# Two small edits to a fused attention and MLP kernel: a cast layout for whole-array transposes, and a second PSUM tile for one A@V

## The chip, the cores and the metric

The kernel runs on one core of one Trainium2 chip. The metric is device time in microseconds (us). It varies from one execution to the next, so it is given as a median with the range. The span in a profile, first to last instruction, is 1.8 us shorter than the device time of the same execution (390.1 against 391.87 for the profiled execution of the kernel before).

Names: PE is TensorE, PEld its weight loads, DVE is VectorE, ACT is ScalarE, POOL is GpSimd, SP is the engine that issues most DMAs. PSUM is the memory that holds the tiles PE writes in this kernel, and from which DVE and ACT copy them; such a copy is called an eviction. Tiles in the profile: `qraw` and `qe` are q before and after its cast, `tps` its transposes, `sc` and `sch` scores, `av` and `avh` the product A@V of attention and v, `xT` that product scaled, `hps` and `ops` the two MLP layers. The chain is the work that ended last, followed back from wait to wait; a load lands when its data has arrived.

## The reference

```python
scores = scale * q @ k.T                  # 8 batches, 12 heads, 448 positions, 64 wide
attn   = maximum(scores, 0)**2 / 448
x      = (attn @ v), heads side by side   # 3584 x 768
h      = x @ w_in                         # 768 x 2048
g      = maximum(h, 0) + alpha * minimum(h, 0)
out    = g @ w_out                        # 2048 x 768
```

## The kernel before

The heads are worked on four at a time, as 24 "quads" (three to a batch). Two heads lie on partitions 0 to 63 and two on 64 to 127; the index `s` tells the two heads of a partition half apart. Scores are computed transposed, so q and k of a quad are first turned by PE (quads 0 to 5) or by a DMA (the rest).

The opening: q and k of quad 0 are loaded as fp32, cast on DVE and ACT, turned, and the first scores follow. Quads 1 to 5, and quad 0's v, are loaded with a casting DMA from POOL's queue.

```python
raw[(0, w)]  = raw_pool.tile([128, 2, NJ, D], F32, ...)
cast[(0, w)] = early_pool.tile([128, 2, NJ, D], BF16, ...)     # s outside, j inside
...
warm(15)                                     # 15 empty matmuls
nc.vector.tensor_copy(cast[(0, "q")][:, 0], raw[(0, "q")][:, 0])
nc.scalar.copy(cast[(0, "q")][:, 1], raw[(0, "q")][:, 1])
transpose(0, "q")
nc.scalar.copy(cast[(0, "k")][:, :, :3], raw[(0, "k")][:, :, :3])
transpose(0, "k", first, nc.scalar)
warm(2)
nc.vector.tensor_copy(cast[(0, "k")][:, :, 3:], raw[(0, "k")][:, :, 3:])
scores(0, 0); scores(0, 1); scores(0, 2, "both", mm_ps)
```

Inside `transpose`, each j takes two half-width transposes, one per s, which write the two partition halves of PSUM:

```python
for j in js:
    for s in range(2):
        nc.tensor.transpose(ps[64 * s:64 * s + 64, j], t[:, s, j], ident)
```

The end of batch 1's attention: `attnv(5)` multiplies quad 5's attention with v into one PSUM tile, and one ACT instruction scales it into `xT`. Twelve matmuls of the first MLP layer that need only quads 3 and 4 stand ready around it, four of them after it. Then come those that need quad 5.

```python
# in attnv, batch 1 and later
elif isinstance(ps, list):      # two PSUM tiles
    nc.vector.tensor_scalar(xT[b][:, g, 0], half[0][:, :S], out_scale, None, ALU.mult)
    nc.scalar.activation(xT[b][:, g, 1], half[1][:, :S], ACTF.Copy, scale=out_scale)
else:                           # one tile
    nc.scalar.activation(xT[b][:, g], ps[:, :, :S], ACTF.Copy, scale=out_scale)
...
ffn1(1, 0, range(0, 4))
ffn1(1, 1, range(0, 4))
attnv(5)
feed(7, "v")()                  # DVE casts quad 7's v
ffn1(1, 2, range(0, 4))         # the four matmuls that don't need quad 5
for ff in range(3):
    ffn1(1, ff, range(4, KM))   # these need it
```

Of the kernel before, what the change touches and what calls it, by code (L numbers as in the profile page):

```python
# [11 lines left out]
BF16 = mybir.dt.bfloat16  # L12
# [8 lines left out]
NJ = 7  # L21
# [3 lines left out]
def kernel(  # L25
# [10 lines left out]
    nc = tc.nc  # L36
    B, H, S, D = q.shape
    d_model, d_ff = moe_w_in.shape
    assert H * D == d_model and S == PP * NJ and D == 64 and H % 4 == 0
    NG = H // 4  # L40
    n_pe = 2 * NG
# [6 lines left out]
    def pool(name, bufs, **kw):  # L48
        return ctx.enter_context(tc.tile_pool(name=name, bufs=bufs, **kw))
# [6 lines left out]
    early_pool = pool("early", 2)  # L56
# [15 lines left out]
    ident = singles.tile([128, 128], BF16)  # L72
# [4 lines left out]
    raw, cast, qT, kT, vb = {}, {}, {}, {}, {}  # L77
    src = {"q": q, "k": k, "v": v}

    def flat(n, w):  # L80
        b, g = quads[n]
        return src[w][b, 4 * g:4 * g + 4].rearrange("(s hf) (pp j) d -> (hf pp) s (j d)", hf=2, j=NJ)

    def load(n, names="qkv", after=None):
        for w in names:
            t = raw_pool.tile([128, 2, NJ, D], F32, tag=w, name=f"{w}raw")
            raw[(n, w)] = t
            if after is not None:
                nc.gpsimd.tensor_copy(t[:, 0, 0, 0:1], after)
                after = None  # L90
            nc.sync.dma_start(out=t.rearrange("p s j d -> p s (j d)"), in_=flat(n, w))
# [10 lines left out]
    def copy(eng, o, i):  # L102
        if eng is nc.scalar:
            nc.scalar.copy(o, i)  # L104
        else:
            eng.tensor_copy(o, i)  # L106

    def to_bf16(n, w, eng):
        r = raw.pop((n, w))
        if w == "v":  # L110
            t = v_pool.tile([128, 2, NJ, D], BF16, tag="v", name="vb")
            vb[n] = t
            copy(eng, t, r)
        else:
            t = cast_pool.tile([128, NJ, 2, D], BF16, tag=w, name=f"{w}b")
            cast[(n, w)] = t
            copy(eng, t.rearrange("p j s d -> p s j d"), r)

    def transpose(n, w, js=range(NJ), eng=None):
        store = qT if w == "q" else kT  # L120
        if n not in store:
            store[n] = qkT_pool.tile([128, NJ, 2, PP], BF16, tag=w, name=f"{w}T")
        t, dst = cast[(n, w)], store[n]
        if n >= n_pe:
            nc.sync.dma_start_transpose(out=dst.rearrange("p j h c -> p j (h c)"),
                                        in_=t.rearrange("p j s d -> p (j s d)"))
            return
        ps = mm_ps.tile([128, NJ, 2 * PP], BF16, tag="mm", name="tps")
        for j in js:
            for s in range(2):  # L130
                nc.tensor.transpose(ps[64 * s:64 * s + 64, j], t[:, s, j], ident)  # L131
        lo, hi = js[0], js[-1] + 1
        copy(eng or nc.vector, dst[:, lo:hi].rearrange("p j h c -> p j (h c)"), ps[:, lo:hi])
# [54 lines left out]
    def squares(keep=0, single=None):  # L188

        while len(todo) >= 2 + keep or todo and single is not None:  # L190
            m = min(len(todo), 2)
            some = [todo.pop(0) for _ in range(m)]
            t = some[0][2]
            a = at_pool.tile([128, 2, 2, S], BF16, tag="at", name="at")
            if m == 2:
                nc.vector.tensor_tensor(a, t, t, ALU.mult)  # L196
            else:
                cur.clear()
                if single is nc.scalar:
                    nc.scalar.activation(a[:, 0], t[:, 0], ACTF.Square)  # L200
                else:
                    nc.vector.tensor_tensor(a[:, 0], t[:, 0], t[:, 0], ALU.mult)
            for i, (n, j, _) in enumerate(some):
                att[(n, j)] = a[:, i]
# [3 lines left out]
    def attnv(n, js=range(NJ), space=sc_ps, apart=False):  # L208
        b, g = quads[n]
        if js[0] == 0:  # L210
            if space is mm_ps:
                av_ps[n] = [mm_ps.tile([128, 512], F32, tag="mm", name="avh") for _ in range(2)]
            elif apart:
                av_ps[n] = [sc_ps.tile([128, 2, 512], F32, tag="sc", name="av2")[:, 0] for _ in range(2)]
            else:
                av_ps[n] = sc_ps.tile([128, 2, 512], F32, tag="sc", name="av")
        ps = av_ps[n]
        half = ps if isinstance(ps, list) else [ps[:, r] for r in range(2)]
        for j in js:
            a = att.pop((n, j))  # L220
            for r in range(2):
                for s in range(2):
                    nc.tensor.matmul(half[r][64 * s:64 * s + 64, :S],  # L223
                                     vb[n][64 * r:64 * r + 64, s, j, :],
                                     a[64 * r:64 * r + 64, s],
                                     start=(j == 0), stop=(j == NJ - 1))
        if js[-1] != NJ - 1:
            return
        if g == 0:
            xT[b] = xT_pool.tile([128, NG, 2, S], BF16, tag="xT", name="xT")  # L230
        if b == 0:
            nc.scalar.activation(xT[b][:, g, 0], half[0][:, :S], ACTF.Copy, scale=out_scale)  # L232
            if g > 0:
                nc.vector.tensor_scalar(xT[b][:, g, 1], half[1][:, :S], out_scale, None, ALU.mult)
            else:
                nc.scalar.activation(xT[b][:, g, 1], half[1][:, :S], ACTF.Copy, scale=out_scale)
        elif isinstance(ps, list):
            nc.vector.tensor_scalar(xT[b][:, g, 0], half[0][:, :S], out_scale, None, ALU.mult)  # L238
            nc.scalar.activation(xT[b][:, g, 1], half[1][:, :S], ACTF.Copy, scale=out_scale)  # L239
        else:  # L240
            nc.scalar.activation(xT[b][:, g], ps[:, :, :S], ACTF.Copy, scale=out_scale)  # L241
# [62 lines left out]
    def steps(b, what):  # L304
        if what == "in":
            return [(1.12, lambda ff=ff: ffn1(b, ff)) for ff in range(KF)]
        cs = range(0, 3) if b % 2 == 0 else range(3, 7)
        return [(1.3, lambda c=c, hf=hf, h=h: ffn2(b // 2, c, hf, h)) for c in cs for hf in range(2) for h in range(2)]


    NQ = len(quads)
    def group(units, how="both"):

        def f():
            order = sorted(units, key=lambda u: u[1] == "av")
            for i, (n, j) in enumerate(order):
                if j == "av":
                    if (n, NJ - 1) not in att:
                        squares(single=nc.vector)
                    attnv(n)  # L320
                elif i == 0 and len(order) == 3:
                    scores(n, j, how, mm_ps)
                else:
                    scores(n, j)
            squares()
            for n, j in order:
                if n < n_pe:
                    continue
                if j == 0:
                    if n + 2 < NQ:  # L330
                        load(n + 2)
                    if n + 1 < NQ:
                        transpose(n + 1, "k")
                        transpose(n + 1, "q")
                if j == 4 and n > 2 * NG and n + 2 < NQ:
                    for w in "kqv":
                        to_bf16(n + 2, w, nc.gpsimd)
        return f


# [5 lines left out]
    def warm(count):  # L346

        ps = sc_ps.tile([128, 2, 512], F32, tag="sc", name="warm")
        for _ in range(count):
            nc.tensor.matmul(ps[:, 0, :256], warm_w, warm_x, start=True, stop=True)  # L350

    nc.scalar.dma_start(out=alpha_sb, in_=moe_alpha.rearrange("(kf p) -> kf p", p=128))
    for w in "qk":
        raw[(0, w)] = raw_pool.tile([128, 2, NJ, D], F32, tag=w, name=f"{w}raw")
        cast[(0, w)] = early_pool.tile([128, 2, NJ, D], BF16, tag=w, name=f"{w}e")
    first, rest = range(0, 3), range(3, NJ)
    nc.sync.dma_start(out=raw[(0, "q")].rearrange("p s j d -> p s (j d)"), in_=flat(0, "q"))
    for js in (first, rest):
# [10 lines left out]
    load_bf16(0, "v")  # L369
    load_bf16(1, "v")  # L370
    warm(15)
    nc.vector.tensor_copy(cast[(0, "q")][:, 0], raw[(0, "q")][:, 0])
    nc.scalar.copy(cast[(0, "q")][:, 1], raw[(0, "q")][:, 1])
    transpose(0, "q")
    nc.scalar.copy(cast[(0, "k")][:, :, :3], raw[(0, "k")][:, :, :3])
    transpose(0, "k", first, nc.scalar)
    warm(2)
    nc.vector.tensor_copy(cast[(0, "k")][:, :, 3:], raw[(0, "k")][:, :, 3:])
    scores(0, 0)
    scores(0, 1)  # L380
    scores(0, 2, "both", mm_ps)
# [1 line left out]
    ps = mm_ps.tile([128, KF], F32, tag="mm", name="aps")  # L383
# [75 lines left out]
    f = [fn for _, fn in steps(0, "in")]  # L459
# [8 lines left out]

    ffn1(1, 0, range(0, 4))
    ffn1(1, 1, range(0, 4))  # L470
    attnv(5)
    feed(7, "v")()
    ffn1(1, 2, range(0, 4))
    for ff in range(3):
# [107 lines left out]
```

## Time and profile before

| | kernel before |
|---|---|
| device time, 3 executions | 391.43 us (391.19 to 391.59) |
| span in the profile | 390.1 us |
| PE busy, DVE, ACT | 97%, 65%, 55% |
| first matmul of the MLP (hps) starts | 22.22 us |
| last A@V matmul of batch 1 starts | 72.70 us |

The chain and timeline lines that the argument starts from stand in the prediction.

### The profile page before, as it was taken

The numbers are of one execution on the slowest core, as the hardware profiler recorded it, in microseconds if no ns is written. First come the engines' busy times: TensorE is split into PE (matmuls) and PEld (weight loads), VectorE is DVE, ScalarE is ACT, GpSimd is POOL, SyncE is SP. The second block draws the span as 40 slices with busy tenths as digits, with TensorE's granted clock in tenths as the row PEclk, the third lists the DMA queues.
The fourth block names the chain that finished last, engine by engine and source line by source line (L and its number), as shares of the span: only waits on it lengthen the run. The fifth ranks groups of instructions, "written<-read, shape, count | busy, mean of one in ns | idle before, by whom it ended". The sixth has DMA issues, their size and how long they took to land.

```text
span 390.1 us, 7871 instructions
## 1 busy us (share of the span) xinstructions
PE 379.2 (97%) x3210; PEld 215.0 (55%) x3210; DVE 252.1 (65%) x335; ACT 215.6 (55%) x361; POOL 73.3 (19%) x88
## 2 busy tenths in 40 slices
PE   7699999999999999999999999999999999999996
PEld 4345556445665456645665456654566545655564
DVE  3976877587677757766674666777676376725411
ACT  5975767574556656654474645766565365624200
POOL 5664000061241014201231012311030000000000
PEclk9999999999999999999999999999999999999999
DMA  7999997893995528926494354947163220130033
GB/s 155 185 208 205 203 221 271 239 319 83 237 271 184 114 76 232 229 64 165 87 276 141 66 164 96 247 159 172 30 91 85 72 47 2 42 81 2 0 82 81
DMA packets 64755, 55.43 MB, mean 142 GB/s; under 512 B 35776, under 2 KB 60496, under 8 KB 64720
## 3 DMA queue, kind: packets, MB, share of 16 engines
q1 hardware_dynamic: 53472, 44.77, 44.2%
q0 software_dynamic: 10976, 9.96, 16.1%
q8 instruction: 25, 0.41, 0.4%
q10 hardware_dynamic: 272, 0.21, 0.2%
q14 instruction: 10, 0.08, 0.1%
HBM read 45.62 MB, written 11.01 MB: 145 GB/s over the span
## 4 chain that ended last, share of the span: by engine, by line
PE 94%; DMA 3%; ACT 1%; DVE 1%; issue 0%
PE hps L255 37%; PE ops L271 37%; PE avh L223 7%; PE sc L156 6%; PE sch L156 3%; DMA ke<-in_k_dram 2%; PE ops L294 1%; PE tps L131 1%; PE av L223 1%; DMA qraw<-in_q_dram 1%; ACT rl L185 1%; ACT xT L241 0%; DVE gT L263 0%; ACT rl L163 0%; DVE rl L165 0%
## 5 line engine op out<-in xcount | busy, mean ns | idle before, releaser
L255 PE MATMUL hps<-xT,w_in_sb 128*128 128x448 bf16 x768 | 149.3, 353 | 0.8 <-ACT xT L232 0.4
L271 PE MATMUL ops<-w_out_sb,gT 128*128 128x384 bf16 x864 | 145.8, 326 | 0.0
L263 DVE SCALAR_TENSOR_TENSOR gT<-neg,beta_sb,hps 128x448 bf16<-128x448 f32 x128 | 85.7, 679 | 61.1 <-ACT neg L262 60.2
L271 PEld LDWEIGHTS <-gT 128*128 128x128 bf16 x864 | 83.4, 98 | 61.2 <-issue 7.9
L255 PEld LDWEIGHTS <-w_in_sb 128*128 128x128 bf16 x768 | 74.0, 98 | 72.8 <-issue 5.9
L262 ACT ACTIVATE neg<-hps 128x448 f32<-128x448 f32 x128 | 69.0, 545 | 63.8 <-PE hps L255 63.7
L185 ACT ACTIVATE rl<-sc 128x896 bf16<-128x896 f32 x87 | 77.1, 923 | 44.4 <-PE sc L156 44.3
L196 DVE TENSOR_TENSOR at<-rl 128x1792 bf16<-128x1792 bf16 x80 | 85.5, 1112 | 2.1 <-ACT rl L185 0.9
L106 DVE COPY osb<-ops 128x384 f32<-128x384 f32 x30 | 16.7, 557 | 46.0 <-PE ops L271 46.0
L163 ACT ACTIVATE rl<-sch 128x448 bf16<-128x448 f32 x81 | 41.6, 550 | 4.6 <-PE sch L156 4.6
L106 POOL CAST kb<-kraw 128x896 bf16<-128x896 f32 x16 | 18.4, 1152 | 115.2 <-DMA kT<-kb 55.7
L156 PE MATMUL sc<-qT,kT 64*64 64x448 bf16 x456 | 35.9, 355 | 3.8 <-ACT rl L185 1.5
L223 PE MATMUL avh<-at,vb 64*64 64x448 bf16 x588 | 34.2, 350 | 0.0
L156 PEld LDWEIGHTS <-kT 64*64 64x64 bf16 x672 | 21.9, 106 | 20.1 <-issue 13.0
L104 ACT COPY osb<-ops 128x384 f32<-128x384 f32 x24 | 11.4, 475 | 36.0 <-PE ops L271 36.0
L223 PEld LDWEIGHTS <-vb 64*64 64x64 bf16 x672 | 25.6, 106 | 9.3 <-issue 4.9
L183 DVE TENSOR_SCALAR rl<-sc 128x896 bf16<-128x896 f32 x27 | 29.4, 1090 | 0.6 <-PE sc L156 0.6
L106 POOL CAST vb<-vraw 128x896 bf16<-128x896 f32 x16 | 16.8, 1050 | 36.5 <-PE avh L223 36.0
L156 PE MATMUL sch<-qT,kT 64*64 64x448 bf16 x216 | 22.5, 355 | 0.0
L106 POOL CAST qb<-qraw 128x896 bf16<-128x896 f32 x16 | 15.9, 991 | 32.3 <-DMA qT<-qb 32.3
L165 DVE TENSOR_SCALAR rl<-sch 128x448 bf16<-128x448 f32 x27 | 16.8, 622 | 2.6 <-ACT xT L239 0.8
L238 DVE TENSOR_SCALAR xT<-avh 128x448 bf16<-128x448 f32 x19 | 11.9, 625 | 7.7 <-PE avh L223 7.7
(55 smaller groups left out, 96.8 us busy)
## 6 DMA issues: line engine op xcount, KB each, us to landing
out_dram<-osb SPq DMA_DIRECT2D x54, 192.0 KB, 2.7
qraw<-in_q_dram SPq DMA_DIRECT2D x19, 448.0 KB, 5.4
kraw<-in_k_dram SPq DMA_DIRECT2D x18, 448.0 KB, 4.4
vraw<-in_v_dram SPq DMA_DIRECT2D x18, 448.0 KB, 6.3
w_out_sb<-in_moe_w_out_dram POOLq DMA_DIRECT2D x2, 1536.0 KB, 20.0
w_in_sb<-in_moe_w_in_dram POOLq DMA_DIRECT2D x8, 192.0 KB, 8.3
w_in_sb<-in_moe_w_in_dram POOLq DMA_DIRECT2D x4, 384.0 KB, 9.7
vb<-in_v_dram POOLq DMA_DIRECT2D x6, 224.0 KB, 9.7
```

The source lines that it names most:

```text
L106: eng.tensor_copy(o, i)
L156: nc.tensor.matmul(half[r][64 * c:64 * c + 64, :S], kT[n][64 * r:64 * r + 64, j, c, :], qT[n][64 * r:64 * r + 64, :, c, :], start=True, st ...
L163: nc.scalar.activation(rl[:, r], half[r][:, :S], ACTF.Relu)
L165: nc.vector.tensor_scalar(rl[:, r], half[r][:, :S], 0.0, None, ALU.max)
L183: nc.vector.tensor_scalar(rl, ps[:, :, :S], 0.0, None, ALU.max)
L185: nc.scalar.activation(rl, ps[:, :, :S], ACTF.Relu)
L196: nc.vector.tensor_tensor(a, t, t, ALU.mult)
L223: nc.tensor.matmul(half[r][64 * s:64 * s + 64, :S], vb[n][64 * r:64 * r + 64, s, j, :], a[64 * r:64 * r + 64, s], start=(j == 0), stop=(j ...
L255: nc.tensor.matmul(ps, w_in_sb[:, km // 2, km % 2, bass.ts(ff, 128)], xT[b][:, km // 2, km % 2, :], start=(km == 0), stop=(km == KM - 1))
L262: nc.scalar.activation(neg, ps, ACTF.Relu, scale=-1.0)
L263: nc.vector.scalar_tensor_tensor(gT[b // 2][:, ff, (b % 2) * S:(b % 2) * S + S], neg, beta_sb[:, ff:ff + 1], ps, ALU.mult, ALU.add)
L271: nc.tensor.matmul(ps, gT[sb][:, ff, bass.ts(c, 128)], w_out_sb[:, ff, bass.ts(hf, 384)], start=(ff == 0), stop=(ff == KF - 1))
```

## The change

The intent: quad 0's casts write `p j s d` in place of `p s j d`, so that the two s-tiles of one j lie side by side and one 128-wide transpose does what took two of 64. And the last A@V of batch 1 goes into two PSUM tiles, so that DVE and ACT can take one half each. A loop in `group`, which served quads that never reach it, is removed.

```diff
+        if n == 0:
+            t = t.rearrange("p j s d -> p j (s d)")
 ...
         for j in js:
+            if n == 0:
+                nc.tensor.transpose(ps[:, j], t[:, j], ident)
+                continue
             for s in range(2):
 ...
-        cast[(0, w)] = early_pool.tile([128, 2, NJ, D], BF16, ...)
+        cast[(0, w)] = early_pool.tile([128, NJ, 2, D], BF16, ...)
 ...
-    nc.vector.tensor_copy(cast[(0, "q")][:, 0], raw[(0, "q")][:, 0])
-    nc.scalar.copy(cast[(0, "q")][:, 1], raw[(0, "q")][:, 1])
+    nc.vector.tensor_copy(cast[(0, "q")][:, :, 0], raw[(0, "q")][:, 0])
+    nc.scalar.copy(cast[(0, "q")][:, :, 1], raw[(0, "q")][:, 1])
 ...  (both casts of k likewise)
-    attnv(5)
+    attnv(5, apart=True)
```

More of the change, by code (lines that the diff above doesn't have):

```diff
@@ L325, in f @@
             squares()
-            for n, j in order:
-                if n < n_pe:
-                    continue
-                if j == 0:
-                    if n + 2 < NQ:
-                        load(n + 2)
-                    if n + 1 < NQ:
-                        transpose(n + 1, "k")
-                        transpose(n + 1, "q")
-                if j == 4 and n > 2 * NG and n + 2 < NQ:
-                    for w in "kqv":
-                        to_bf16(n + 2, w, nc.gpsimd)
         return f
@@ L354 @@
         raw[(0, w)] = raw_pool.tile([128, 2, NJ, D], F32, tag=w, name=f"{w}raw")
-        cast[(0, w)] = early_pool.tile([128, 2, NJ, D], BF16, tag=w, name=f"{w}e")
+        cast[(0, w)] = early_pool.tile([128, NJ, 2, D], BF16, tag=w, name=f"{w}e")
     first, rest = range(0, 3), range(3, NJ)
@@ L371 @@
     warm(15)
-    nc.vector.tensor_copy(cast[(0, "q")][:, 0], raw[(0, "q")][:, 0])
-    nc.scalar.copy(cast[(0, "q")][:, 1], raw[(0, "q")][:, 1])
+    nc.vector.tensor_copy(cast[(0, "q")][:, :, 0], raw[(0, "q")][:, 0])
+    nc.scalar.copy(cast[(0, "q")][:, :, 1], raw[(0, "q")][:, 1])
     transpose(0, "q")
-    nc.scalar.copy(cast[(0, "k")][:, :, :3], raw[(0, "k")][:, :, :3])
+    nc.scalar.copy(cast[(0, "k")][:, :3].rearrange("p j s d -> p s j d"), raw[(0, "k")][:, :, :3])
     transpose(0, "k", first, nc.scalar)
     warm(2)
-    nc.vector.tensor_copy(cast[(0, "k")][:, :, 3:], raw[(0, "k")][:, :, 3:])
+    nc.vector.tensor_copy(cast[(0, "k")][:, 3:].rearrange("p j s d -> p s j d"), raw[(0, "k")][:, :, 3:])
     scores(0, 0)
```

## The prediction

The sum came to 391.43 - 0.28 + 0.0 = 391.15 us. That DVE's cast of q would grow from 0.43 us to 0.63 in the new layout was the author's estimate. Beside it stood a measured time, 0.62 us for a 448-column DVE pass out of PSUM in the trace of the kernel before. What is said of a change of tiling rests on one measurement: 0.28 us from the last av matmul (64x64) to the next hps matmul (128x128), against 0.189 between two hps matmuls.

> **What bounds the kernel now.** I read the page first (busy shares, chain, groups), then the chain in order of time, then the timeline around the two places that the change touches.
>
> The page's busy shares and its chain by engine:
>
> ```profile
> PE 379.2 (97%) x3210; PEld 215.0 (55%) x3210; DVE 252.1 (65%) x335; ACT 215.6 (55%) x361; POOL 73.3 (19%) x88
> ...
> PE 94%; DMA 3%; ACT 1%; DVE 1%; issue 0%
> ```
>
> TensorE is busy 97% and holds 94% of the chain. The same matmuls run after the change, so only a wait of PE, or a switch between its tilings, can be won. The granted clock is 1.00, so nothing is to be had there. The groups of the stretch from 74.1 us on show no idle time of PE before any group but the one wait at 74.07 itself: everything there is back to back. So a wait removed before 74.1 us should arrive at the end whole, and one moved into a place where PE waits for something else should not arrive at all.
>
> The chain in order of time shows the two places. Columns: start us, length us, what.
>
> ```profile
> 0.74 3.87 DMA qraw<-in_q_dram
> 4.61 0.02 issue
> 4.63 0.44 DVE qe L372
> 5.07 0.04 issue
> 5.12 0.99 PE tps L131 x20
> 6.10 0.02 issue
> 6.13 0.49 ACT kT L104
> ...
> 8.31 7.40 DMA ke<-in_k_dram
> 15.71 0.04 issue
> 15.76 0.58 PE tps L131 x14
> ...
> 71.60 1.48 PE av L223 x28
> 73.08 0.02 issue
> 73.10 0.93 ACT xT L241
> 74.03 0.04 issue
> 74.07 3.00 PE hps L255 x15
> ```
>
> The first is quad 0's cast and transposes, which the change rewrites. But the chain then goes through the load of quad 2's keys, landing at 15.71. The second is the last A@V of batch 1: its result leaves PSUM in one ACT instruction of 0.92 us, and PE's next-but-four matmul waits for it.
>
> The timeline of the second place (start us, us, engine, line, operation, then idle before and who ended it):
>
> ```profile
> 72.98 0.93 PE L255 MATMUL hps<-xT,w_in_sb 128*128 128x448 bf16 x4
> 73.10 0.92 ACT L241 ACTIVATE xT<-av 128x896 bf16<-128x896 f32 x1 [3.42 <-PE av L223]
> ...
> 74.07 1.49 PE L255 MATMUL hps<-xT,w_in_sb 128*128 128x448 bf16 x7 [0.16 <-ACT xT L241]
> ```
>
> PE has only four matmuls that don't need this result. The page counts 0.16 us idle, but that is measured from the modelled end of a pipelined matmul. A matmul of 448 columns in a stream follows its predecessor after 0.189 us (96 of them in one run take 18.16 us later in the same chain: 0.189). Four from 72.98 (the first gap is 0.20) let the fifth start at 73.75. It starts at 74.07. The real loss is **0.32 us**.
>
> [...]
> - [...] The trace has such a stream, the last 128-column pieces of the output, each with its own 128x128 load: 10 in 0.72 us with 219 ns for one, so (0.72 - 0.22) / 9 = 55.7 ns. [...]
> - [...] the 14 half-width transposes take 0.58 us, which is 7 pairs at 56 ns (below), so the two column halves already run at once. [...] between the last av matmul and the first hps about 0.09 us is lost beyond the normal pitch.
> [...]
>
> **Part 1: quad 0's layout.** What it removes: 14 of 28 transposes with their loads. Does it remove time? Timeline of such transposes now and of full-width 128-column matmuls:
>
> ```profile
> 8.82 0.58 PE L131 MATMUL tps<-ident,ke 128*64 128x128 bf16 x14
> ...
> 385.60 0.72 PE L294 MATMUL ops<-w_out_sb,gT 128*128 128x128 bf16 x10
> ```
>
> Seven full-width ones at 55.7 ns with 20 ns of start-up like the present ones take 6 x 0.0557 + 0.02 + 0.22 = 0.57 us; the 14 half-width ones take 0.58. So the instruction count halves and **PE's time does not**. The first q pair now starts half at 5.12 (DVE's half) and half at about 5.25 (ACT's); the rest stream from 5.25. The merged ones start when both halves are cast, 5.25, and end the same.
>
> What it adds: [...] I choose 0.63. It then ends at 5.26, not 5.06, against ACT's half at 5.20: the transposes of q start 0.06 late. q's copy to SBUF would end at 6.55 in place of 6.49; the k side (ACT cast to 5.67, three pairs of transposes, ACT copy to 6.61) ends later than that and barely moves (up to 0.03 us, if the q transposes push the k ones). ACT's casts cost the same in either layout (961 strided, 966 plain, for 128x896). The rest of k, cast by DVE with an even split, has 0.4 us of room. So the first score starts at 6.66 to 6.69. The switch of tiling before the two warm-up matmuls goes, 0.1 us, but the scores behind them wait for kT anyway.
>
> And whatever comes of it meets the wait for quad 2's keys:
>
> ```profile
> 14.00:16.00 2.00, 1.42 (x36) 0.89 (x26) 1.90 (x3) 2.00 (x5) 0.00 (x1) 1.00 1.22 191
> ...
> 15.76 0.58 PE L131 MATMUL tps<-ident,ke 128*64 128x128 bf16 x14 [0.58 <-DMA ke<-in_k_dram]
> ```
>
> The first line is the stretch 14 to 16 us (busy PE, PEld, DVE, ACT, POOL, clock, DMA share, GB/s): the DMA engines are full, so that transfer lands when the queue reaches it, not 7.4 us after its issue. PE waits 0.58 us there, and so stands ready to absorb up to that much delay, and to swallow any gain. **Part 1: 0.0 us**, give or take 0.1.
>
> **Part 2: two PSUM tiles.** Removed: one ACT pass of 917 ns. Added: DVE 625 ns and ACT 543 ns at the same time (the means of the groups of other batches that leave PSUM in halves). DVE starts a little behind PE's end, 0.04 after ACT in the one place of the kernel before where two tiles of this pool are used (26.56 and 26.60): 73.12 + 0.625 = 73.75, and 0.04 for the semaphore gives 73.79 for the fifth matmul, in place of 74.07. Gain **0.28 us**; 0.04 of the 0.32 us stays. Second PSUM tile: its last reader, a score pass at 67.9 + 0.95 = 68.9 us, is done long before 71.53, so nothing waits. DVE is idle from 71.6 to 75.2; the cast of quad 7's v, which it does now at 70.97, moves behind the eviction to about 73.75 to 74.37. Its buffer is asked for again by the load issued at about 75.98, so that doesn't wait either.
>
> **Part 3: the loop taken out of the grouped scores** handled only quads from 6 on, and the groups are called with quads 3 to 5 alone. It never ran: 0.
>
> **Sum:** 391.43 - 0.28 + 0.0 = **391.15 us**.
>
> **The rivals.**
> - The start counts after all. For it: the chain does name the first cast and transposes. Against: seven pairs cost what seven full ones do, and the load at 15.71 hides the rest. If it held and some 0.3 us fell away there as well: 390.85.
> - The DVE cast slows down and this is not absorbed, because DVE is nearly without gaps from 7.5 to 16.5 us (1.90 of 2.00 in the stretch above). [...] Against: 0.58 us of PE's waiting comes after it, and the k side sets the first score. It would give back up to 0.2: 391.35.
> - The stall at 74 us only changes its name: half the result now waits on DVE, and if DVE's eviction began late (behind a cast) PE would wait for DVE as it did for ACT. For it: two casts and an output copy sit in DVE's queue just before. Against: they end by 71.1. It would make 391.4.
>
> **Range and chances.** Three runs before span 0.40 us, larger than the effect, so the measured median may be 0.2 either way; the rivals reach from 390.85 to 391.4. I choose 390.7 to 391.6. Two per cent would be 7.8 us; all that the changed code touches on the path is under 2 us. Within 2%: 0.98, the other two 0.01 each.
>
> **What would show it.** Right: the fifth hps matmul after the last av of batch 1 waits for DVE, under 0.1 us, and what follows lies some 0.28 us earlier to the end; the seven-transpose groups take about 0.57 us; the q cast on DVE takes 0.6 us or more; quad 2's keys still land near 15.7. Wrong: those keys landing clearly earlier or later, seven transposes in 0.35 us or in 0.75, PE idle anew after 74 us, or a span that moves by more than 0.6 us.

## More of the kernel before

PE is the engine that everything waits for, but not from the start: until 22 us the scores wait for loads, casts and for the copies out of PSUM. From there on it runs nearly without gaps (busy 363.7 of the 367.9 us that are left). One row of the page matters later. In it each digit is the granted TensorE clock, in tenths, of one fortieth of the span (9.75 us):

```profile
PEclk9999999999999999999999999999999999999999
```

No slice is below 9. The row, and the mean clock that is given for each execution below, leave out the start, though: the clock records begin at 4.16 us here, and before that the empty matmuls of 256 columns follow each other after 0.213 us, against 0.120 us for the pair at 6.02. So neither shows a slow start.

## The result

| | before | after |
|---|---|---|
| device time, 6 executions each | 391.36 us (391.17 to 391.85) | 391.42 us (390.98 to 393.20) |
| ratio of the means, 95% interval | | 1.0008 (0.9988 to 1.0028) |
| span of the profiled execution | 390.1 us | 391.3 us |

The ratio is the mean time of one kernel's fast executions over that of the other's of the same rounds, so it is not quite the ratio of the medians. All executions here count as fast (none is 1.5% above the fastest).

The medians agree, and yet the six executions of the changed kernel hold 390.98, which is under every one of the kernel before, and 393.20 and 392.22, which are above. The profiled one is the 393.20. So the first question is what happened in that execution. The same row of its page as above, and the chain by engine:

```profile
PEclk9699999999999999999999999999999999999999
...
PE 95%; DMA 2%; ACT 1%; POOL 0%; issue 0%; DVE 0%
```

The second slice has a 6: for part of it PE's clock was halved. The clock records of the trace say it exactly: 0.5 from 11.11 to 17.94 us, 6.83 us long. The same 28 A@V matmuls of quad 0 (timeline: start us, us, engine, line, operation, count), in the kernel before:

```profile
13.66 1.52 PE L223 MATMUL avh<-at,vb 64*64 64x448 bf16 x28
```

and in the changed kernel:

```profile
14.12 2.88 PE L228 MATMUL avh<-at,vb 64*64 64x448 bf16 x28
```

They take nearly twice as long. Nothing in the diff touches them. The chain of the changed kernel, in order of time:

```profile
4.88 5.58 DMA qe<-in_q_dram
10.46 0.04 issue
10.50 0.58 PE tps L136 x14
...
14.39 2.61 PE avh L228 x27
...
73.19 1.45 PE av L228 x28
74.64 3.71 PE hps L260 x19
```

Two things differ from the chain that the prediction shows. The load of quad 2's keys is not on it (here they landed at 14.76, not 15.71). The load of quad 1's q is: it landed at 10.46, against 9.67 in the kernel before. And after the last A@V of batch 1 no ACT piece follows: PE goes from av to hps without waiting. That place in the timeline:

```profile
74.57 2.26 PE L260 MATMUL hps<-xT,w_in_sb 128*128 128x448 bf16 x11
74.68 0.62 DVE L243 TENSOR_SCALAR xT<-av 128x448 bf16<-128x448 f32 x1 [2.04 <-PE av L228]
74.72 0.54 ACT L244 ACTIVATE xT<-av 128x448 bf16<-128x448 f32 x1 [3.44 <-PE av L228]
```

Eleven hps matmuls stream without a gap where before four were followed by a wait. From the first to the fifth it is 0.780 us in the trace, and it was 1.087. The gain of part 2, 0.307 us, is there.

The cast of quad 0's q in the kernel before, then the cast and the transposes in the changed one:

```profile
4.63 0.43 DVE L372 CAST qe<-qraw 128x448 bf16<-128x448 f32 x1 [3.56 <-DMA qraw<-in_q_dram]
...
4.60 0.62 DVE L365 CAST qe<-qraw 128x448 bf16<-128x448 f32 x1 [3.52 <-DMA qraw<-in_q_dram]
...
5.36 0.55 PE L133 MATMUL tps<-ident,qe 128*128 128x128 bf16 x7 [0.91 <-DVE qe L365]
```

DVE's cast takes 0.62 us in place of 0.43, and the seven transposes take 0.55, where fourteen took 0.58 once streaming.

**The span as a sum.** The two traces can be cut at three points that both have: the first hps matmul, the last A@V matmul of batch 1, and the first and fifth hps matmuls after it.

| | before | after |
|---|---|---|
| start to first hps | 22.22 | 23.81 |
| first hps to last av | 50.48 | 50.48 |
| last av to next hps | 0.28 | 0.28 |
| that hps to the fifth | 1.087 | 0.780 |
| fifth to the end | 316.01 | 315.99 |
| span | 390.08 | 391.34 |

Only two rows differ: the fourth, by the gain of part 2, and the first, by 1.59 us. That first row holds quad 0's layout, but also the halved clock and the later landing of quad 1's q. The experiments have to tell whether the change made it.

### The profile page after: what moved, and what is told of

Same layout as the page of the kernel before. It is cut to its first block, busy times and chain, and to the rows that moved or that the text cites. A ratio compares the mean times of both kernels' runs of the same rounds, so it can differ in the third digit from the quotient of the medians.

```text
span 391.3 us, 7845 instructions
## 1 busy us (share of the span) xinstructions
PE 381.6 (98%) x3196; PEld 215.7 (55%) x3196; DVE 251.5 (64%) x336; ACT 215.5 (55%) x361; POOL 71.0 (18%) x88
## 4 chain that ended last, share of the span: by engine, by line
PE 95%; DMA 2%; ACT 1%; POOL 0%; issue 0%; DVE 0%
PE hps L260 37%; PE ops L276 37%; PE avh L228 8%; PE sc L161 6%; PE sch L161 3%; DMA qe<-in_q_dram 1%; PE ops L299 1%; PE tps L136 1%; PE av L228 1%; ACT rl L190 1%; DMA alpha_sb<-in_moe_alpha_dram 1%; ACT rl L168 0%; POOL ke L360 0%; DVE gT L268 0%; ACT xT L237 0%
## 5 line engine op out<-in xcount | busy, mean ns | idle before, releaser
L201 DVE TENSOR_TENSOR at<-rl 128x1792 bf16<-128x1792 bf16 x80 | 84.1, 1093 | 2.1 <-ACT rl L190 0.9
L161 PE MATMUL sc<-qT,kT 64*64 64x448 bf16 x456 | 37.0, 363 | 2.5 <-ACT rl L190 1.2
L228 PE MATMUL avh<-at,vb 64*64 64x448 bf16 x588 | 35.5, 360 | 0.0
L106 POOL CAST vb<-vraw 128x896 bf16<-128x896 f32 x16 | 15.0, 939 | 35.4 <-PE avh L228 35.2
```

What stands on the lines that cost most here:

```text
L106: eng.tensor_copy(o, i)
L161: nc.tensor.matmul(half[r][64 * c:64 * c + 64, :S], kT[n][64 * r:64 * r + 64, j, c, :], qT[n][64 * r:64 * r + 64, :, c, :], start=True, st ...
L201: nc.vector.tensor_tensor(a, t, t, ALU.mult)
L228: nc.tensor.matmul(half[r][64 * s:64 * s + 64, :S], vb[n][64 * r:64 * r + 64, s, j, :], a[64 * r:64 * r + 64, s], start=(j == 0), stop=(j ...
```

## The experiments

Sixteen kernels ran, in four groups of four; those of a group ran on the same chip and share its executions of the kernel before.

### The two kernels again, and each part alone

e1 is the kernel before with no edit, e2 the changed kernel with no edit. e3 is the changed kernel with `attnv(5)` in place of `attnv(5, apart=True)`. e4 is the kernel before with this:

```diff
-    attnv(5)
+    attnv(5, apart=True)
```

> Control: the kernel before, run as an experiment so that span and clock of each execution are listed. Theory A (the long profiled execution of the changed kernel, 391.3 us at clock 0.99, was a halved TensorE clock between 11.1 and 17.9 us that came by chance of how the first loads landed): a share of these executions is also at clock 0.99 and about 1.2 to 1.6 us longer than the rest. Theory B (the new cast layout makes it): none is. Executions at clock 1.00 have a span of about 390.1.

> The changed kernel again. At clock 1.00 its span is 389.8 (0.3 below the control) if the second PSUM tile's gain arrives at the end. Theory A: clock 0.99 no oftener than in the control, and then 391.3. Theory B: 0.99 in a third of the executions or more. A rival for the gain (it is given back later): span at clock 1.00 equal to the control's within 0.1.

> Only quad 0's layout; last A@V of batch 1 in one tile as before. My step: 0.0 us at clock 1.00, span 390.1, the stall before the fifth hps matmul still 0.32 us, q's DVE cast 0.62 us. Theory B: clock 0.99 as often as the whole change. Rival (start counts): 0.2 to 0.3 us shorter than the control.

> Only the two PSUM tiles. Span at clock 1.00: 389.8, 0.3 us under the control; the fifth hps matmul starts 0.78 us after the first in place of 1.09. Theory B: no execution at 0.99. Rival (given back): 390.1.

| | median us (range) | ratio to before (95%) | spans in order |
|---|---|---|---|
| before, 11 executions | 392.49 (391.53 to 393.57) | | 389.7 to 391.8 |
| e1 before again | 392.43 (391.18 to 393.83) | 1.0000 (0.9974 to 1.0026) | 389.4 389.6 390.1 391.2 391.3 392.0 |
| e2 after again | 392.83 (391.62 to 393.58) | 1.0011 (0.9989 to 1.0034) | 389.8 390.7 390.8 391.1 391.7 391.7 |
| e3 part 1 only | 391.84 (391.29 to 394.15) | 0.9997 (0.9971 to 1.0024) | 389.5 389.8 389.9 390.2 391.2 392.4 |
| e4 part 2 only | 391.43 (391.21 to 393.65) | 0.9993 (0.9966 to 1.0020) | 389.3 389.4 389.5 389.6 390.9 391.8 |

On this chip the kernel before scatters as widely as the changed one, by over 2 us. Its profiled execution, e1, has the halved clock itself:

```profile
PEclk9899999999999999999999999999999999999999
```

So theory B, that the new layout makes it, falls as the only cause: the unchanged kernel does it, and part 2 alone, which leaves quad 0 as it was, has an execution at mean clock 0.991 as well. Nor do the counts show it more often with the new layout: a mean clock of 0.996 or less is in 3 of 12 executions with it (2 of 6 of e2, 1 of 6 of e3) and in 5 of 23 without (4 of 17 of the kernel before, 1 of 6 of e4).

The halved clock is not all of the scatter on this chip. Of the 18 executions above 392.3 us, 10 have a mean clock of 0.998 or 1.000, among them the longest of e1 (393.83). So the expectations of e1 and e2, spans of about 390.1 and 389.8 at clock 1.00, held for some executions only. Those ten were not profiled, and their cause is open; a slow start before the clock records would not show in their means (the profiled e13 has 1.000, though its records begin only at 6.00 us).

What comes before a halving can be read from the traces for a stretch as long as the shorter halved time. In the changed kernel PE was busy 2.02 of the 3.41 us before its clock fell (7.70 to 11.11), and the longest single wait that the timeline shows there is 0.79 us. In e1 it was busy 1.44 of the 3.41 us before (10.50 to 13.91). The kernel before kept its clock after a stretch of the same length with only 1.69 us (10.99 to 14.40). So the profile's busy time alone doesn't part the traces that were halved from those that were not, and no limit is drawn from it.

Part by part, the local expectations held: e3's stall before the fifth hps matmul is unchanged (1.087 us from the first to the fifth), e4's is gone (0.781), and in all four profiles the rest of the program after the fifth takes 316.01 to 316.03 us. The gain of part 2 is not given back.

### Keeping PE busy in the opening

The author's hypothesis, theory A in the texts of e5 and e8, was that too little work on PE brings the halved clock. If so, empty work should prevent it. e5 adds 20 empty matmuls of 256 columns where PE waits for data, into PSUM tiles that the next real work overwrites; e6 is the same on the changed kernel.

```diff
+    def fill(ps, count):
+        for _ in range(count):
+            nc.tensor.matmul(ps[:, :256], warm_w, warm_x, start=True, stop=True)
+    fills = {(0, 3): 4, (1, 0): 8}
 ...  in scores:
+        fill(half[0], fills.get((n, j), 0))
         score_mm(n, j, half, rs)
 ...  in transpose:
+        if (n, w) in ((1, "q"), (2, "k")):
+            fill(ps.rearrange("p j c -> p (j c)").bitcast(F32), 4)
```

e7 adds to e6 a swap of the two evictions and another split of q's cast:

```diff
-            nc.vector.tensor_scalar(xT[b][:, g, 0], half[0][:, :S], ...)
-            nc.scalar.activation(xT[b][:, g, 1], half[1][:, :S], ...)
+            first, second = (1, 0) if n == 5 else (0, 1)
+            nc.vector.tensor_scalar(xT[b][:, g, first], half[first][:, :S], ...)
+            nc.scalar.activation(xT[b][:, g, second], half[second][:, :S], ...)
 ...
-    nc.vector.tensor_copy(cast[(0, "q")][:, :, 0], raw[(0, "q")][:, 0])
-    nc.scalar.copy(cast[(0, "q")][:, :, 1], raw[(0, "q")][:, 1])
+    nc.vector.tensor_copy(cast[(0, "q")][:, :4] (as p s j d), raw[(0, "q")][:, :, :4])
+    nc.scalar.copy(cast[(0, "q")][:, 4:] (as p s j d), raw[(0, "q")][:, :, 4:])
```

e8 goes the other way. It is the kernel before with one load made late, so that PE waits for it:

```diff
-    load_bf16(1, "q")
     load_bf16(0, "v")
     load_bf16(1, "v")
+    load_bf16(1, "q")
```

> The kernel before with 20 empty 256-column matmuls added at four places of the first 16 us where PE waits for data (into PSUM tiles that the next real work overwrites). Theory A [...]: no execution under clock 0.998, spans within 0.5 us of each other, near 389.6 to 390.1. Rival (the clock is halved for another reason, or the long starts are the loads' alone): the same scatter of 389.4 to 392.0 as the control.

> The changed kernel with the same 20 fillers. If the gain of the second PSUM tile arrives whole and only the start's scatter hid it: the median is 0.3 us below that of the kernel before with fillers, spans within 0.5 us of each other. Rival (quad 0's layout lengthens the start): equal or longer than it.

> As the one before, with two more edits: the half that the fifth hps matmul reads leaves PSUM on ACT (543 ns) and the other on DVE, and the casts of quad 0's q are split by j (DVE 4 rows times 2, ACT 3 times 2) [...]. Expected: fifth hps matmul 0 to 0.02 us earlier; DVE's q cast 0.42 us for 512 columns in place of 0.62 for 448. [...] Total within 0.1 us of the one before.

> The kernel before with one order changed: quad 1's q is loaded after the two v loads, so it lands near 12.5 us in place of 9.7 [...]. Theory A: clock 0.991 to 0.996 in nearly every execution, matmuls of the next 3.4 or 6.8 us at half speed, spans 391 to 393. Rival (clock does not depend on it): clock 1.00 and a span longer by what PE waits, some 0.5 to 2 us, with all matmuls at full speed.

| | median us (range) | ratio to before (95%) | spans | mean clock |
|---|---|---|---|---|
| before, 11 executions | 392.63 (391.22 to 394.00) | | 389.4 to 392.2 | 0.991 to 0.999 |
| e5 before, 20 fillers | 391.93 (391.64 to 392.33) | 0.9985 (0.9963 to 1.0007) | 389.9 to 390.5 | 1.000 in all 6 |
| e6 after, 20 fillers | 391.74 (391.41 to 392.03) | 0.9977 (0.9953 to 1.0001) | 389.5 to 390.2 | 1.000 in all 6 |
| e7 swap and 8-row cast | 391.97 (391.57 to 393.07) | 0.9991 (0.9966 to 1.0015) | 389.7 to 391.2 | 0.998 to 1.000 |
| e8 q late | 395.63 (395.38 to 395.82) | 1.0078 (1.0051 to 1.0105) | 393.6 to 394.0 | 0.991 in all 4 |

On this chip that accounts for the long executions, from both sides. All six plain ones with a span of 390.8 or more have a mean clock of 0.996 or 0.991, the five others 0.998 or more. With fillers alone (e5, e6) the range shrinks from 2.8 us to 0.7 and 0.6, and no execution has the halved clock. With the late load (e8) all four executions have a mean clock of 0.991. It doesn't account for the ten long ones of the chip before. And e6 lies 0.19 us under e5 in the median, where 0.3 was expected. The timeline of e8's PE, with idle times in brackets:

```profile
9.26 0.38 PE L156 MATMUL sc<-qT,kT 64*64 64x448 bf16 x4
13.07 0.96 PE L131 MATMUL tps<-ident,qe 128*64 128x128 bf16 x14 [3.43 <-DMA qe<-in_q_dram]
```

PE waits 3.43 us for the late q. Then the transposes take 0.96 us in place of 0.58: the clock was halved at 12.53, and stayed so for 6.83 us. e8's expected span (391 to 393) was too low by 0.6 to 1.0 us. That the wait and the slow stretch add would explain it, but no run parts them.

Of e7, the swap did what it should: 0.765 us from the first to the fifth hps matmul, against 0.780. DVE's cast, now 8 rows of 64 in place of 7, gained less than expected:

```profile
4.30 0.53 DVE L374 CAST qe<-qraw 128x512 bf16<-128x512 f32 x1 [3.22 <-DMA qraw<-in_q_dram]
```

It took 0.53 us for 512 columns where 0.42 was expected (k's cast of 512 columns takes 0.42 in the kernel before). q's cast of 448 columns took 0.39 to 0.49 us in the ten traces of the old layout, and 0.62 in all seven of the new one with 7 rows. But a cast of one shape varies by itself: k's, a little later, took 0.42 us in most traces and 0.67 in e2 and e10. So one trace of e7 doesn't show whether the number of rows is what costs, and why the times vary is not settled. e7's total missed its expectation (within 0.1 us of e6): two of its six executions had a span of 391.2 at mean clock 1.000. They were not profiled, so their cause is open; the same fillers were in them, so fillers don't remove every long start.

### Can the parts be told apart in the total?

e9 to e12 are before, after, part 1 only and part 2 only, each with the 20 fillers and a longer opening block. The edit, beside those above:

```diff
-    warm(15)
+    warm(18)
```

> The kernel before with the 20 fillers and three more empty matmuls in the opening block (18 in place of 15), so that PE is busy until the first cast is done. In the earlier runs the profile's first full-clock record began between 3.8 and 7.1 us[...]. All executions at clock 0.998 or more, spans within 0.6 us, median about 391.9.

> The whole change on the same quiet start. Theory (only part 2 counts): 0.31 us less than e9_before_quiet in the median, give or take 0.15. Rival (the layout costs or saves at the start as well): 0.1 or 0.6 less.

> Only quad 0's layout on the quiet start. Theory: equal to e9_before_quiet within 0.15 us, the stall before the fifth hps matmul still 0.32 us. Rival: 0.2 us or more longer (the slower q cast on DVE) or shorter (fewer transposes).

> Only the two PSUM tiles on the quiet start. Theory: 0.31 us less than e9_before_quiet, give or take 0.15, and equal to e10_after_quiet. Rival (given back): equal to e9_before_quiet.

| | median us (range, 5 executions) | mean us | ratio to before (95%) |
|---|---|---|---|
| before, 9 executions | 391.40 (391.15 to 393.02) | 391.59 | |
| e9 before, quiet | 391.74 (391.70 to 392.46) | 391.93 | 1.0013 (1.0001 to 1.0026) |
| e10 after, quiet | 391.74 (391.41 to 392.02) | 391.75 | 1.0009 (0.9996 to 1.0021) |
| e11 part 1, quiet | 391.88 (391.68 to 392.41) | 391.95 | 1.0014 (1.0001 to 1.0028) |
| e12 part 2, quiet | 391.94 (391.52 to 392.36) | 391.90 | 1.0012 (1.0000 to 1.0025) |

The expected 0.31 us below e9 is not seen: e10's median equals e9's and e12's lies 0.20 above it. The order of the means (e9 and e11 above e10 and e12) is the expected one, but the differences are smaller than the scatter: inconclusive. Two things came of it. The fillers and the longer block cost something themselves: on this chip, where only 1 of 9 plain executions was long, e9 was 0.3 us slower than the kernel before. And the longer opening block didn't do its work in e10. Its clock records began only at 6.33 us, and q's transposes, before that, were slow:

```profile
5.17 0.91 PE L135 MATMUL tps<-ident,qe 128*128 128x128 bf16 x7
```

These seven transposes took 0.91 us in place of 0.55, and the first score came 2.58 us after q's landing in place of 2.08.

### Lighter fillers, and one tile with two evictions

e13 to e15 are before, after and part 2 only with 12 fillers in place of 20:

```diff
-    fills = {(0, 3): 4, (1, 0): 8}
+    fills = {(0, 3): 2, (1, 0): 5}
 ...
-            fill(ps..., 4)
+            fill(ps..., 3 if n == 1 else 2)
```

e16 has the kernel before with those 12, and leaves A@V of quad 5 in one PSUM tile, but takes it out as two halves:

```diff
+        elif n == 5:
+            nc.vector.tensor_scalar(xT[b][:, g, 0], half[0][:, :S], out_scale, None, ALU.mult)
+            nc.scalar.activation(xT[b][:, g, 1], half[1][:, :S], ACTF.Copy, scale=out_scale)
         else:
             nc.scalar.activation(xT[b][:, g], ps[:, :, :S], ACTF.Copy, scale=out_scale)
```

> The kernel before with 12 fillers in place of 20 (2 before the score pass of quad 0's j=3, 5 before quad 1's first scores, 3 and 2 before the transposes of quad 1's q and quad 2's k). The 20 fillers made the way from the first score to the first hps matmul 15.65 us, against 15.40 and 15.56 in two executions without: they cost 0.1 to 0.25 us themselves. With 12: 15.4 to 15.5, and still no halved clock; median about 391.6, spread under 1 us.

> The whole change with 12 fillers. Theory (only part 2 counts): 0.31 us under e13_before_light, about 391.3, in the mean; in its profile the fifth hps matmul 0.78 us after the first, and the end 316.0 us after that. Rival (layout costs at the start): equal to e13_before_light.

> Only the two PSUM tiles, with 12 fillers. Theory: as e14_after_light within the scatter (0.2 us in the mean of five). Rival (layout saves at the start): 0.2 us or more longer than e14_after_light.

> The last A@V of batch 1 stays in one PSUM tile, but leaves it as two halves on DVE and ACT at once. If the second tile is not what gains, but the two evictions side by side: fifth hps matmul 0.78 us after the first, as with two tiles. Rival (the readers of one tile wait for each other): 1.1 us or more, as before or worse.

| | median us (range) | ratio to before (95%) |
|---|---|---|
| before, 11 executions | 391.56 (391.20 to 393.11) | |
| e13 before, light | 392.26 (391.38 to 392.43) | 1.0007 (0.9991 to 1.0022) |
| e14 after, light | 391.33 (391.11 to 393.88) | 1.0001 (0.9980 to 1.0023) |
| e15 part 2, light | 391.35 (391.25 to 392.29) | 0.9996 (0.9982 to 1.0011) |
| e16 one tile, light | 391.79 (391.59 to 392.86) | 1.0008 (0.9991 to 1.0026) |

e14 and e15 have the lowest medians, and e13 lies above them by more than the theory asks, but one execution of e14 (393.88, mean clock 1.000, not profiled) undoes its mean. So the lighter fillers don't remove every long start, and no version is shown to beat the kernel before in the total. e13 missed its own expectation (391.6, within 1 us). Its profiled execution is a long one at mean clock 1.000, and its timeline shows where 0.8 us went:

```profile
16.95 0.58 PE L133 MATMUL tps<-ident,qe 128*64 128x128 bf16 x14 [0.43 <-DMA qe<-in_q_dram]
```

Its clock records began only at 6.00 us, the first score came 2.34 us after q's landing (0.2 to 0.3 us late), and PE waited for quad 2's q, which landed at 16.91. From the first score to the first hps matmul it is 15.73 us, against 15.24 in e14, e15 and e16.

e16 is clear, from its timeline:

```profile
72.62 0.62 DVE L249 TENSOR_SCALAR xT<-av 128x448 bf16<-128x448 f32 x1 [2.05 <-PE av L231]
...
73.28 0.54 ACT L250 ACTIVATE xT<-av 128x448 bf16<-128x448 f32 x1 [4.08 <-DVE xT L249]
73.88 0.92 PE L266 MATMUL hps<-xT,w_in_sb 128*128 128x448 bf16 x4 [0.23 <-ACT xT L250]
```

With one tile ACT's half does not start (73.28) until DVE's has ended (73.24). The fifth hps matmul is early (0.797 us after the first), but the sixth waits for ACT until 73.88, and from the fifth to the end it takes 316.42 us in place of 316.01. The one wait has become another, 0.1 us worse in sum than the kernel before. So it is with the second PSUM tile that the two evictions run side by side in this program (in e4 ACT starts 0.04 us after DVE).

### Where each profiled execution spent its opening

All of these are read from the traces. "q" is when quad 0's q has landed, "full clock from" when the clock records begin, "score" the first score matmul, "q1" the landing of quad 1's q, "halved" the time at half clock.

| | layout | full clock from | q | score, after q | q1 | halved | score to first hps |
|---|---|---|---|---|---|---|---|
| before | old | 4.16 | 4.61 | 2.05 | 9.67 | 0 | 15.56 |
| after | new | 4.28 | 4.57 | 2.08 | 10.46 | 6.83 | 17.15 |
| e1 | old | 7.08 | 4.23 | 2.48 | 9.37 | 3.41 | 16.70 |
| e2 | new | 6.64 | 4.24 | 2.58 | 9.57 | 3.41 | 16.44 |
| e3 | new | 4.83 | 4.49 | 2.08 | 11.12 | 6.83 | 17.91 |
| e4 | old | 5.05 | 4.31 | 2.06 | 9.68 | 0 | 15.40 |
| e5 | old | 3.85 | 4.29 | 2.10 | 9.25 | 0 | 15.65 |
| e6 | new | 4.90 | 4.28 | 2.08 | 10.55 | 0 | 16.28 |
| e10 | new | 6.33 | 4.39 | 2.58 | 9.32 | 0 | 15.65 |
| e11 | new | 4.12 | 4.51 | 2.08 | 9.18 | 0 | 15.65 |
| e12 | old | 3.97 | 4.56 | 2.12 | 10.65 | 0 | 16.06 |
| e13 | old | 6.00 | 4.52 | 2.34 | 9.89 | 0 | 15.73 |
| e14 | new | 3.99 | 4.37 | 2.08 | 9.31 | 0 | 15.24 |
| e15 | old | 4.07 | 4.51 | 2.11 | 9.21 | 0 | 15.24 |

From the first hps to the last av it is 50.48 or 50.49 us in each of the 18 traces. So in these traces the scatter of the span is made before the first hps matmul, by five things: when q lands (4.23 to 4.67 us), whether the full clock has begun by then (up to 0.5 us), when quad 1's q lands (over 10 us costs 0.4 to 0.9 in e6, e7 and e12), when quad 2's load lands (e13, 0.5), and whether the clock is halved (about 1 us for 3.41 us of it; 6.83 us of it and a late q1 together cost 1.6 to 2.5, and no trace without fillers has one of those two alone).

## Why the prediction was right or wrong

**Part 2, the two tiles: right.** It gave 0.28 us; 0.307 was measured, in every one of the eight traces with both tiles and the plain order of evictions (0.780 to 0.782 from the first to the fifth hps matmul). The stall left was 0.012 us in place of 0.04, because DVE began 0.036 us after the end of the A@V, earlier than I had taken from the other place. Nothing of it is lost later: 315.98 to 316.03 us (in those eight) from the fifth matmul to the end. The third rival (the stall changes its name) was wrong for two tiles. It is what happens with one tile, in e16.

**Part 1, the layout, as a cost: right.** DVE's cast took 0.62 us (0.63 predicted), seven transposes 0.55 (0.57 predicted), and the first score came at 6.65 us (6.66 to 6.69 predicted). With the full clock on time the old layout gives a first score 2.03 to 2.12 us after q's landing, and the new one 2.08 each time. So, with the clock on time, halving the number of transposes gains nothing, and the slower cast costs nothing. With a late clock the new layout shows 2.58 (e2, e10) and the old one 2.32 to 2.48 (e8, e13, e1), which are too few to tell.

**Part 1, the absorber: wrong.** The step that failed is "And whatever comes of it meets the wait for quad 2's keys". I read the landing at 15.71 as fixed by a full queue, and the 0.58 us of PE's waiting there as a cushion. In the other 17 traces those keys landed between 13.41 and 14.76 us, and that wait had gone; in two of them (e4 and e13) PE waited 0.42 and 0.43 us for quad 2's q instead. Keys landing clearly earlier, and a span that moved by more than 0.6 us (by 1.26), were signs of being wrong that the prediction itself had named. The opening is instead a chain from the first score to the first hps matmul. With q1 on time it is 15.65 us long in each of the 20-filler traces (e5, e10 and e11 in the table, and e9), however late the first score is: there a late first score goes straight into the total. Where q1 is late, as in the changed kernel's profile, the chain starts with that load, and a late score would hide behind it. It did no harm to the forecast for part 1 itself, because its 0.0 didn't need the cushion.

**The range and the total: wrong.** The step that failed is "Three runs before span 0.40 us, larger than the effect, so the measured median may be 0.2 either way". A change of -0.28 us was forecast, and the medians differ by +0.06. The three executions were all short ones. Among 11 executions of the same kernel on another chip the range was 391.2 to 394.0. The mean of the changed kernel's six lies above the range because one of them, at 393.20, had a halved clock for 6.83 us and a late q1, together worth 1.59 us at the first hps matmul; another, 392.22 at mean clock 1.000, was not profiled. None of my rivals named it: I wrote "The granted clock is 1.00, so nothing is to be had there", which was true of that one execution (from 4.16 us on) and not of the kernel. The six profiles without fillers, three of each, show the clock halved in one of three of the old layout (e1, not the kernel before or e4) and in three of three of the new one (after, e2, e3). That is more on the new side, while the mean clocks of all executions on that chip are alike (3 of 12 and 5 of 23), so a small effect of the layout on how often it occurs is neither shown nor excluded.

So the expected gain of 0.3 us is in the kernel and stays in it; it is smaller than what chance makes of the first 22 us, and can't be seen in medians of six.

## What to carry to other kernels

Before forecasting an effect of some tenths of a per cent, look at how one kernel's executions differ from each other, and cut the span at points that every trace has: here two cuts turned a scatter of 2 us into one row that varies and several that agree to 0.03 us. An opening in which the matmul engine is partly idle deserves its own check of the clock, in several executions (here 8 of the 35 in the first group of experiments had a mean of 0.996 or less), and in the trace, since the mean leaves out what lies before the first clock record (4.16 us of it in the kernel before). A wait that one profile shows need not be there in the next: the one for quad 2's keys, 0.58 us in the kernel before, had gone in the other 17 traces. And here half as many instructions gained nothing: fourteen half-width transposes took 0.58 us, seven full-width ones 0.55.
